# Attention and an MLP in one instruction stream: S2 and S1 score pairs placed one by one between pieces of MLP

## The chip, the cores and the metric

The kernel runs on one core of a Trainium2 chip. The metric is the device time of one execution in microseconds (us). A second time stands beside it: the span, from the first to the last instruction that the hardware profiler recorded in one profiled execution.

The engines are called as in the profile: PE is TensorE (PEld its weight loads, which overlap its matmuls), DVE is VectorE, ACT is ScalarE, POOL is GpSimd, SP is SyncE, which issues most DMAs. Each engine works through its own instruction stream in order; they wait for one another by semaphores.

## The reference, cut to what matters

```python
x: 1 x 2048 x 576 (float32), H = 32 heads of Dh = 18, F = 4608
g = sigmoid((x * gate_w).sum(-1, keepdims=True))

qkv = x @ wqkv                       # 576 -> 3 * 576
scores = q @ k.T * Dh ** -0.5        # per head 2048 x 2048
p = softmax(scores)
a = (p @ v) merged over heads @ wo   # 576 -> 576

y = layernorm(x)
h = gelu(y @ w1 + b1)                # 576 -> 4608, tanh form of gelu
b = h @ w2 + b2                      # 4608 -> 576

out = g * a + (1 - g) * b
```

All matrices are float32. The kernel keeps precision by splitting values into a high part (type fp32r) and the rest; a product is then three matmuls, high by high, high by low and low by high, added up in one PSUM bank.

## The kernel before, in words

There are three stages. First, x is transposed and normalised, and q, k, v are computed and written to DRAM scratch with their high and low parts (up to about 250 us). Second, one long loop does all of attention and, in its gaps, all of the MLP. Third, the output projection with `wo` runs in the gaps of the loop's last steps and after it (from about 2230 us).

**Attention in the loop.** A unit is one pair of heads and one half of the 2048 queries: 32 units. A step is one unit and one block of 128 keys: 16 steps a unit, 512 steps. The loop at line 1113 runs over units and steps. Each step does, twice, for the two blocks of 512 queries:

- S2 (`s2`, matmul at line 250): the scores of 128 keys by 512 queries for both heads, two matmuls on the two halves of PE's rows at once, a *pair*. ACT takes the exponential of each (line 253) into one of three tiles of p (`RING`).
- S1 (`next_round`, `s1_round`, matmul at line 210): a pair of score blocks with queries in the rows, for the *next* unit, of which DVE takes the row maximum (line 212). The maxima enter the next unit's S2 as extra rows of q. S1 runs one unit and 8 rounds ahead, so the last unit has none.

After every second step `pv` (line 268) multiplies the p of two steps by v: 16 matmuls that use PE as four column groups. So two steps, a *double step*, hold four S2 pairs, four S1 pairs and one PV, and there are 256 double steps.

S2 and S1 take their PSUM banks from one round of five (`score_bank`, line 106). Every pair takes two. Numbered in the order of issue, a pair's first bank was the second bank of the pair three before it, and its second bank the first bank of the pair two before it. S2 and S1 alternate, so an S1 waits on its first bank for the exponentials of the S2 three pairs back, and an S2 on its first bank for the reduces of the S1 three pairs back.

**The MLP in the gaps.** The MLP is a Python generator (`mlp`, line 321). It works through 36 groups: 4 blocks of 512 tokens by 9 groups of 512 hidden columns. A group is two `h_pair`s and four `out_pair`s.

- `h_pair` (line 436) computes 2 x 128 hidden columns for 512 tokens: 27 pairs of matmuls (line 460), one on each row half. Then ACT and POOL do the GELU by steps that `defer` and `queue_end` put off (lines 480 to 514).
- `out_pair` (line 518) adds a group's part of the output for 128 tokens: 24 pairs of matmuls (line 538) into two banks of 288 columns. In the first 12 pairs (turn 0) row half 0 writes bank 0 and half 1 writes bank 1; in the last 12 (turn 1) they change banks. Between the turns, the first matmul of turn 1 must not start before the last two of turn 0 have ended. This is done by the `token`: a tiny activation on ACT (line 547) that waits for those two, and for which the first matmul of turn 1 waits. DVE then adds the banks to the accumulator (line 556).

Both generators yield after every matmul pair and set `cut` where a piece ends. `atom` (line 636) takes one piece. `fill` (line 1096) is called three times a double step, with a share of 0, 1 or 2, and takes one piece each time; `piece[0]` tells the generator in which of the three gaps it stands, and the set `ends` holds the pair counts at which it cuts. In `h_pair`, `last` marks the one before a group's outputs; it is stretched over two double steps. `behind` compares the MLP work done (`spent`) with what should be done by this step (`TOTAL`, `FIN`), so that the MLP ends near step 500.

**The order of everything else.** `run_due` (line 143) advances a model clock (`now`) and a call counter (`slot`) and issues what is due: deferred activations, POOL work, DMA issues. It is called eight times in a double step. Nothing is reordered afterwards: the order in which Python emits the instructions is the order on each engine.

In a double step PE gets: S2 S1 PV, S2 S1, gap 0, S2 S1, gap 1, S2 S1, gap 2. `GAP` (1130 ns) is the least time by which the model clock advances in a gap. After the MLP, `fill` calls `filler` with `FILL` (1100 ns) of the projection's matmuls in each gap. `out_proj` issues its preparations at the steps in `PSTEP`, among them `normed` (line 989), DVE and ACT work on the first block of attention outputs, one stage a `run_due` call.

Of the kernel before, what the change touches and what calls it, by code (L numbers as in the profile page):

```python
# [8 lines left out]
F32 = mybir.dt.float32  # L9
# [18 lines left out]
G = 4  # L28
# [12 lines left out]
LAND = 8  # L41
GAP = 1130.0
BUSY = 20
# [17 lines left out]
def gated_mix_kernel(ctx: ExitStack, tc: tile.TileContext, x, wqkv, wo, w1, b1, w2, b2, gate_w, out):  # L61
    nc = tc.nc
# [68 lines left out]
    def defer(n, fn):  # L131
        later.append((slot[0] + n, fn))
# [188 lines left out]
    def mlp():  # L321
# [102 lines left out]
        open_pairs = [0]  # L424
        token = const.tile([1, 1], F32, name="token")

# [9 lines left out]
        def h_pair(q, last, inner=False):  # L436
# [14 lines left out]
            loaded = 0  # L451
            late = spent[0] < behind[0]
            ends = cuts(27, (5, 5, 4)[piece[0]] if last else (3, 5, 4)[piece[0]])
            if last and piece[0] == 0 and not late:

                ends = {4, 9, 14, 18, 23}
            for k, (w_, s_, c) in enumerate(slots):
# [60 lines left out]
        def out_pair(i, t, acc):  # L518
# [4 lines left out]
            ps = [psum(ps_w) for _ in range(2)]  # L523
            ends = {6, 12} if piece[0] == 0 else {12}
            k = 0
            ends_at, seen = [], []
            for turn in range(2):
                for j in ORDER:
                    while (i, j) not in HT:
                        cut[0] = 3  # L530
                        yield 0
                    hh, hl = HT[i, j]
                    w_ = ready(W2, (i * (G // 2) + j // 2, j % 2))
                    for h_, p_ in ((hh, 0), (hh, 1), (hl, 0)):
                        for h in (0, 1) if turn == 0 else (1, 0):
                            r = slice(64 * h, 64 * h + 64)
                            nn = h ^ turn
                            mm = nc.tensor.matmul(ps[nn][:, :ND], h_[r, tok], w_[p_][r, cs[nn]],  # L538
                                                  start=(k == 0), stop=(k == 6 * G - 1))
                            if k == 3 * G - 1:  # L540
                                ends_at.append(mm)
                            elif k == 3 * G:
                                behind_of(mm, seen[0])
                        k += 1
                        if k == 3 * G:

                            seen.append(nc.scalar.activation(token, ident[:1, :1], AF.Copy))  # L547
                            for mm in ends_at:
                                behind_of(seen[0], mm)
                        if k < 6 * G:  # L550
                            if k in ends:
                                cut[0] = 1
                            yield 131
# [76 lines left out]
    cut = [0]  # L630
    piece = [0]
    behind = [0.0]
    hidden = [-1]
# [271 lines left out]
    def out_proj():  # L905
# [134 lines left out]
        for c in range(7):  # L1040
            defer(c, lambda c=c: normed(0, c))
        yield 0
# [52 lines left out]

    def fill(step, share):

        if over[0] is None and not stream and kept[0] == NT and step > PSTEP[-1] + 1:
            stream.append(proj)
            over[0] = step  # L1100
            spent[0] = 0.0
        if over[0] is None:
            piece[0] = share
            behind[0] = base + (TOTAL - base) * step / FIN
            t = spent[0]
            atom()
            run_due(max(spent[0] - t, GAP))
        else:
            filler(spent[0] + FILL)
            run_due()  # L1110

    looped[0] = True
    for u in range(NU):
        for kc in range(NT):
# [17 lines left out]
            s2(u, kc, 0)  # L1132
            next_round()
            run_due(462.0)
            if kc % 2:
                fill(step, 1)
            elif step > 0:
# [4 lines left out]
            s2(u, kc, 1)  # L1142
            next_round()
            run_due(462.0)
            fill(step, 2 if kc % 2 else 0)
    pv(NSTEP - 2)
# [28 lines left out]
```

## Time and profile before

| | |
|---|---|
| time of three runs, us | 2324.1, 2324.93, 2325.55; median 2324.93 |
| profiled execution | 2325.55 us; span 2323.8 us; mean granted clock of PE 0.996 |
| busy time: PE, PEld | 2292.7 us (99%), 1544.4 us (66%) |
| DVE, ACT, POOL | 1664.8 us (72%), 1441.9 us (62%), 967.7 us (42%) |
| S2 matmuls (line 250) | 2048, 454.7 us busy |
| S1 matmuls (line 210) | 2048, 457.9 us busy |
| PV matmuls (line 268) | 2736 and 1360, 345.0 and 179.1 us busy |
| MLP matmuls (lines 460 and 538) | 3888 and 4352 + 2176 (+ 384), 510.4 and 466.3 + 333.8 us busy |
| row maxima on DVE (line 212) | 2048, 1314.8 us, 685 ns each |
| exponentials on ACT (line 253) | 2048, 740.6 + 368.2 us, 594 ns each |
| token on ACT (line 547) | 144, median 202 ns |

How to read it: busy time is the time in which at least one instruction of the group was in its engine. On PE a matmul counts from its start to a modelled end, also while it waits for its weights, so 99% does not say that PE was at its peak; the distances between the starts of matmuls do. A pair of matmuls on the two row halves shows as x2 in a list by time. "idle before" is the time the engine stood before an instruction, with what ended it. The granted clock is the share of full speed at which the throttle let PE run.

### The profile page before, as it was taken

How to read it: one execution, taken by the hardware profiler on the slowest of the kernel's cores; microseconds unless marked ns; L12 is line 12 of the kernel's file. 1: busy time of each engine (PE TensorE's matmuls, PEld its weight loads, DVE VectorE, ACT ScalarE, POOL GpSimd, SP SyncE). 2: the span in 40 equal slices, each digit the busy share in tenths (PEclk: the TensorE clock that was granted, in tenths of full speed). 3: DMA queues.
4: the chain of work that ended last, by engine and by line, in shares of the span. 5: the costliest groups of instructions: out<-in, count | busy, mean ns of one | idle time of the engine just before them, and what ended most of it. 6: DMA issues, size and time to landing. Idle time of an engine off the chain costs nothing.

```text
span 2323.8 us, 51438 instructions
## 1 busy us (share of the span) xinstructions
PE 2292.7 (99%) x20585; PEld 1544.4 (66%) x20585; DVE 1664.8 (72%) x2890; ACT 1441.9 (62%) x2773; POOL 967.7 (42%) x965
## 2 busy tenths in 40 slices
PE   8998999999999999999999999999999999999999
PEld 7876666666666666666666666666666666666658
DVE  5665677777777777777777777777777777777734
ACT  4222577777776666666676666666666666666662
POOL 4001466666564433333353444444434333333700
PEclk9999899999999999999999999999999999999999
DMA  7747855444456524243263424242364233242264
GB/s 245 244 149 232 232 171 147 149 140 146 137 190 167 159 96 118 99 138 111 77 172 136 157 96 130 88 136 96 118 162 152 96 111 107 97 146 96 77 210 161
DMA packets 165022, 330.31 MB, mean 142 GB/s; under 512 B 57190, under 2 KB 84490, under 8 KB 154054
## 3 DMA queue, kind: packets, MB, share of 16 engines
q1 hardware_dynamic: 163162, 323.76, 44.3%
q8 instruction: 162, 2.65, 0.5%
q10 hardware_dynamic: 1620, 3.26, 0.4%
q14 instruction: 78, 0.64, 0.1%
HBM read 234.16 MB, written 96.58 MB: 142 GB/s over the span
## 4 chain that ended last, share of the span: by engine, by line
PE 92%; DVE 3%; DMA 2%; ACT 1%; issue 1%; SPq 1%; POOL 0%; ACTq 0%; DVEq 0%; POOLq 0%
PE ps L268 20%; PE ps L538 20%; PE ps L460 20%; PE ps L250 13%; PE ps L210 12%; PE ps L1071 3%; PE ps L784 3%; PE ps L805 2%; DVE m L212 1%; DMA qk_scr<-hh 1%; DMA p<-in_A_wqkv_dram 0%; PE ps L711 0%; ACT p L253 0%; DMA x<-in_B_w_dram 0%; DVE x L773 0%
## 5 line engine op out<-in xcount | busy, mean ns | idle before, releaser
L212 DVE TENSOR_REDUCE m<-ps 128x1 f32<-128x512 f32 x2048 | 1314.8, 685 | 393.7 <-PE ps L210 372.2
L253 ACT ACTIVATE p<-ps 128x512 f32<-128x512 f32 x1368 | 740.6, 594 | 372.2 <-PE ps L250 361.9
L166 POOL TENSOR_SCALAR zz<-zz 128x512 f32<-128x512 f32 x288 | 178.6, 620 | 819.1 <-ACT zz L513 802.9
L460 PE MATMUL ps<-big,w 64*128 64x512 f32 x3888 | 510.4, 393 | 0.1
L253 ACT ACTIVATE ring<-ps 128x512 f32<-128x512 f32 x680 | 368.2, 594 | 187.6 <-PE ps L250 182.9
L538 PE MATMUL ps<-w,hh 64*128 64x288 f32 x4352 | 466.3, 299 | 4.0 <-ACT token L547 3.5
L210 PE MATMUL ps<-ka,qa 54*128 54x512 f32 x2048 | 457.9, 422 | 11.0 <-DVE hl L736 6.5
L250 PE MATMUL ps<-qa,ka 56*128 56x512 f32 x2048 | 454.7, 423 | 0.7 <-DVE m L212 0.4
L460 PEld LDWEIGHTS ps<-big,w 64*128 64x128 f32 x3888 | 371.4, 185 | 82.3 <-ACT z L481 0.4
L538 PEld LDWEIGHTS ps<-w,hh 64*128 64x128 f32 x4352 | 370.7, 186 | 45.5 <-ACT token L547 17.3
L166 POOL TENSOR_TENSOR zz<-zz,z 128x512 f32<-128x512 f32 x288 | 371.7, 1291 | 24.0
L250 PEld LDWEIGHTS ps<-qa,ka 56*128 56x128 f32 x2048 | 204.3, 184 | 216.6 <-DVE m L212 180.8
L268 PE MATMUL ps<-p,vt 128*32 128x512 f32 x2736 | 345.0, 599 | 0.0
L538 PE MATMUL ps<-w,hl 64*128 64x288 f32 x2176 | 333.8, 293 | 0.0
L210 PEld LDWEIGHTS ps<-ka,qa 54*128 54x128 f32 x2048 | 206.6, 186 | 110.6 <-ACT p L253 42.4
L166 POOL TENSOR_TENSOR w<-x,w 128x576 fp32r<-128x576 f32 (+1 forms) x54 | 98.3, 1836 | 307.2 <-DMA qk_scr<-hh 172.2
L538 PEld LDWEIGHTS ps<-w,hl 64*128 64x128 f32 x2176 | 215.5, 185 | 0.3 <-POOL hl L166 0.3
L166 POOL TENSOR_TENSOR hl<-zz,hh 128x512 fp32r<-128x512 f32 x136 | 176.6, 1299 | 11.3
L268 PE MATMUL ps<-ring,vt 128*32 128x512 f32 x1360 | 179.1, 598 | 0.0
L268 PEld LDWEIGHTS ps<-p,vt 128*32 128x32 f32 x2736 | 71.5, 109 | 161.2 <-issue 153.9
L556 DVE SCALAR_TENSOR_TENSOR x<-ps,x 128x288 f32<-128x288 f32 x256 | 105.1, 452 | 57.3 <-PE ps L538 57.3
L784 PE MATMUL ps<-big,wqk 128*128 128x512 f32 x432 | 109.7, 402 | 1.5 <-POOL wqk L706 1.4
(101 smaller groups left out, 1394.0 us busy)
## 6 DMA issues: line engine op xcount, KB each, us to landing
w<-w_scr SPq DMA_DIRECT2D x54, 1152.0 KB
w<-w_scr SPq DMA_DIRECT2D x108, 576.0 KB
x<-in_B_w_dram SPq DMA_DIRECT2D x72, 288.0 KB
w_scr<-w SPq DMA_DIRECT2D x18, 1152.0 KB
w_scr<-w SPq DMA_DIRECT2D x36, 576.0 KB
big<-y_scr SPq DMA_DIRECT2D x42, 384.0 KB
qa<-qk_scr SPq DMA_DIRECT2D x192, 72.0 KB
ka<-qk_scr SPq DMA_DIRECT2D x84, 144.0 KB
```

The lines of the kernel that those rows point to most:

```text
L166: fn(*args, **kw)
L210: nc.tensor.matmul(ps, qa[r0:r0 + 54, t * P:(t + 1) * P], ka[r0:r0 + 54, kb * TB:(kb + 1) * TB], start=True, stop=True)
L212: nc.vector.tensor_reduce(M4[u][:, h, t, kb:kb + 1], ps, axis=AX.X, op=ALU.max)
L250: nc.tensor.matmul(ps[h], ka[r0:r0 + 56, kc * P:(kc + 1) * P], qa[r0:r0 + 56, qb * TB:(qb + 1) * TB], start=True, stop=True)
L253: nc.scalar.activation(RING[n % 3][:, qb, h], ps[h], AF.Exp, scale=SCALE)
L268: nc.tensor.matmul(OB[u][r:r + 32, :], v[:, k, 19 * h:19 * h + 32], RING[c % 3][:, qb, h, :], start=(k == 0), stop=(k == NT - 1))
L460: nc.tensor.matmul(ps[h], wt[w_][r, c, :], Y[s_][r, c, :], start=(k == 0), stop=(k == 26))
L538: mm = nc.tensor.matmul(ps[nn][:, :ND], h_[r, tok], w_[p_][r, cs[nn]], start=(k == 0), stop=(k == 6 * G - 1))
L556: nc.vector.scalar_tensor_tensor(dst, ps[nn][:, :ND], 0.5, b2b[:, cs[nn]] if g == 0 else dst, op0=ALU.mult, op1=ALU.add)
L784: nc.tensor.matmul(ps, w_[:, c, ms], big[:, s_, :], start=(k == 0), stop=False)
L805: nc.tensor.matmul(ps[:, :ND], big[:, s_, tok], w_[:, c, cs], start=(k == 0), stop=False)
L1071: nc.tensor.matmul(ps[:, :ND], OT[b][2][:, s_, tok], w_part(w_, c)[:, cs], start=(k == 0), stop=(k == 13))
```

## The change

A gap now lies behind every S2 and every S1 pair except the S1 before PV and the S2 and S1 at the turn, so S2 and S1 no longer follow each other directly. A double step has seven gaps, 0 to 6. PE gets: S2, gap 6, S1, PV, S2, gap 0, S1, gap 1, S2, gap 2, S1, gap 3, S2, gap 4, S1, gap 5, and S2, gap 6 again. A new `half_round` does a gap, an S1 round and `run_due`; it stands where `next_round` and `run_due` stood.

An output pair is cut after 3, 6, 12, 18 and 21 of its 24 matmul pairs and skips gap 3 (`skip`), so that the gaps from 0 on hold 3, 3, 6, 0, 6, 3, 3 pairs. The turn lies where gap 3 is empty: an S1 and an S2 pair stand between the turns. Without S1 rounds (the last unit) the cuts are 6, 12, 16, 20 and gaps 2 and 3 are skipped. An output pair that begins in a later gap is cut evenly. An h_pair takes the gaps that are left in its double step, and seven more where it is `last` and the MLP isn't late, or where it doesn't begin in gap 0.

The token is replaced by a semaphore of its own, `swap`: ACT increments it with an instruction that computes nothing and that waits for the last two matmuls of turn 0; PE waits for its value before turn 1 with an instruction of its own.

`run_due` is still called eight times in a double step: in each of the four `half_round`s, after PV, and after gaps 1, 3 and 5. `since` holds the MLP work done up to the last odd gap, by which the model clock is advanced; `GAP` becomes 1000. In `out_proj`, each stage of the first block's `normed` comes three calls later.

```diff
-GAP = 1130.0
+GAP = 1000.0
+GAPS = 7
+TURNS = (3, 6, 12, 18, 21)
+TAIL = (6, 12, 16, 20)
...
-        token = const.tile([1, 1], F32, name="token")
+        swap = tc.alloc_semaphore("swap")
+        swaps = [0]
...
-            late = spent[0] < behind[0]
-            ends = cuts(27, (5, 5, 4)[piece[0]] if last else (3, 5, 4)[piece[0]])
-            if last and piece[0] == 0 and not late:
-
-                ends = {4, 9, 14, 18, 23}
+            left = GAPS - piece[0]
+            skip.clear()
+            if (last and spent[0] >= behind[0]) or left < GAPS:
+                left += GAPS
+            ends = cuts(27, left)
...
-            ends = {6, 12} if piece[0] == 0 else {12}
+            skip.clear()
+            if piece[0]:
+                ends = cuts(24, GAPS - piece[0]) | {12}
+            elif rounds:
+                ends = set(TURNS)
+                skip.add(3)
+            else:
+                ends = set(TAIL)
+                skip.update((2, 3))
             k = 0
-            ends_at, seen = [], []
+            ends_at = []
             for turn in range(2):
+                if turn == 1:
+                    nc.tensor.wait_ge(swap, swaps[0])
...
                             if k == 3 * G - 1:
                                 ends_at.append(mm)
-                            elif k == 3 * G:
-                                behind_of(mm, seen[0])
                         k += 1
                         if k == 3 * G:
 
-                            seen.append(nc.scalar.activation(token, ident[:1, :1], AF.Copy))
+                            seen = nc.scalar.sem_inc(swap, 1)
+                            swaps[0] += 1
                             for mm in ends_at:
-                                behind_of(seen[0], mm)
+                                behind_of(seen, mm)
...
-            defer(c, lambda c=c: normed(0, c))
+            defer(c + 3, lambda c=c: normed(0, c))
...
-    def fill(step, share):
+    def fill(step, gap):
...
-            piece[0] = share
+            piece[0] = gap
             behind[0] = base + (TOTAL - base) * step / FIN
-            t = spent[0]
-            atom()
-            run_due(max(spent[0] - t, GAP))
-        else:
+            if gap not in skip:
+                atom()
+        elif gap % 2:
             filler(spent[0] + FILL)
-            run_due()
+            since[0] = spent[0]
+        if gap % 2:
+            run_due(max(spent[0] - since[0], GAP))
+            since[0] = spent[0]
+
+    def half_round(step, gap):
+
+        fill(step, gap)
+        next_round()
+        run_due(462.0 + spent[0] - since[0] if gap == GAPS - 1 else 462.0)
+        if gap == GAPS - 1:
+            since[0] = spent[0]
...
             s2(u, kc, 0)
-            next_round()
-            run_due(462.0)
+            half_round(step, 2 if kc % 2 else GAPS - 1)
             if kc % 2:
-                fill(step, 1)
+                fill(step, 3)
             elif step > 0:
                 pv(step - 2)
                 while ROWS:
                     ROWS.pop(0)()
                 run_due(2080.0)
             s2(u, kc, 1)
-            next_round()
-            run_due(462.0)
-            fill(step, 2 if kc % 2 else 0)
+            half_round(step, 4 if kc % 2 else 0)
+            fill(step, 5 if kc % 2 else 1)
```

More of the change, by code (lines that the diff above doesn't have):

```diff
@@ L631, in gated_mix_kernel @@
     piece = [0]
+    skip = set()
+    since = [0.0]
     behind = [0.0]
@@ L1100, in fill @@
             over[0] = step
-            spent[0] = 0.0
+            spent[0] = since[0] = 0.0
         if over[0] is None:
-            piece[0] = share
+            piece[0] = gap
             behind[0] = base + (TOTAL - base) * step / FIN
-            t = spent[0]
-            atom()
-            run_due(max(spent[0] - t, GAP))
-        else:
+            if gap not in skip:
+                atom()
+        elif gap % 2:
             filler(spent[0] + FILL)
-            run_due()
+            since[0] = spent[0]
[8 more added lines that the diff above has]
+            since[0] = spent[0]
     looped[0] = True
```

## The prediction

> **What bounds the kernel now.** I read the page first, then TensorE's weight loads and what they waited for, then seven double steps in a row by window, then one double step instruction by instruction. "PEld" is a weight load, "idle before" the time its unit stood.
>
> ```profile
> span 2323.8 us, 51438 instructions
> PE 2292.7 (99%) x20585; PEld 1544.4 (66%) x20585; DVE 1664.8 (72%) x2890; ACT 1441.9 (62%) x2773; POOL 967.7 (42%) x965
> ```
>
> TensorE bounds the span, but its 99% counts a matmul that stands in the pipe behind a late weight load. Losses must be read from the distances between starts. These are the waits of weight loads from 300 to 2200 us:
>
> ```profile
> PEld ps L210 <- ACT p L253: 41.5, 159, 1.4
> PEld ps L210 <- ACT ring L253: 18.7, 73, 0.3
> ...
> PEld ps L538 <- ACT token L547: 12.5, 64, 0.3
> ...
> PEld ps L210 <- DVE m L212: 5.1, 14, 0.4
> ```
>
> S1 (L210) waits for the exponentials of the S2 pair before it (L253): five score banks go round, S2 and S1 take two each, so S1's first bank is the second bank of the S2 three pairs earlier. The exchange token (L547) is next. VectorE hardly holds TensorE. Seven consecutive double steps (a whole group of MLP: h_pair in one step, h_pair in two, four output steps):
>
> ```profile
> 2082.30:2092.51 10.21, 10.21 (x88) 6.91 (x87) 5.72 (x11) 4.51 (x9) 0.00 (x0) 1.00 0.56 221
> 2092.51:2099.74 7.23, 7.23 (x63) 4.41 (x61) 6.23 (x10) 6.81 (x14) 4.92 (x6) 1.00 0.25 67
> 2099.74:2106.83 7.09, 7.09 (x60) 4.22 (x58) 5.27 (x9) 4.64 (x9) 6.48 (x7) 1.00 0.49 186
> 2106.83:2114.21 7.38, 7.38 (x82) 5.00 (x81) 5.99 (x12) 6.78 (x15) 5.20 (x6) 1.00 0.45 161
> 2114.21:2121.66 7.45, 7.45 (x82) 5.00 (x80) 5.90 (x12) 4.50 (x10) 6.18 (x7) 1.00 0.06 22
> 2121.66:2129.18 7.52, 7.52 (x83) 5.01 (x81) 5.87 (x12) 4.51 (x10) 0.00 (x0) 1.00 0.01 2
> 2129.18:2136.69 7.51, 7.51 (x82) 5.01 (x81) 6.21 (x15) 4.49 (x10) 0.00 (x0) 1.00 0.00 0
> ```
>
> Columns: length, then busy us of PE, PEld, DVE, ACT, POOL, then granted clock (1.00), DMA share, GB/s. An output step takes 7.38 to 7.52 us, mean 7.465, whatever POOL and DMA do; DVE is busy 5.9 to 6.2 us of it, ACT 4.5 to 6.8. Inside the step from 2121.66, TensorE's starts:
>
> ```profile
> 2121.31 0.43 PE L210 MATMUL ps<-ka,qa 54*128 54x512 f32 x2
> 2121.66 1.06 PE L268 MATMUL ps<-ring,vt 128*32 128x512 f32 x8
> ...
> 2123.52 0.50 PE L250 MATMUL ps<-qa,ka 56*128 56x512 f32 x2
> 2123.86 0.40 PE L210 MATMUL ps<-ka,qa 54*128 54x512 f32 x2
> 2124.09 0.43 PE L538 MATMUL ps<-w,hh 64*128 64x288 f32 x4
> ...
> 2124.89 0.40 PE L250 MATMUL ps<-qa,ka 56*128 56x512 f32 x2
> 2125.25 0.50 PE L210 MATMUL ps<-ka,qa 54*128 54x512 f32 x2
> 2125.59 0.43 PE L538 MATMUL ps<-w,hh 64*128 64x288 f32 x4
> ...
> 2126.25 0.30 PE L538 MATMUL ps<-w,hl 64*128 64x288 f32 x2
> 2126.38 0.40 PE L250 MATMUL ps<-qa,ka 56*128 56x512 f32 x2
> 2126.61 0.41 PE L210 MATMUL ps<-ka,qa 54*128 54x512 f32 x2
> 2126.90 0.54 PE L538 MATMUL ps<-w,hh 64*128 64x288 f32 x4
> ...
> 2128.59 0.42 PE L250 MATMUL ps<-qa,ka 56*128 56x512 f32 x2
> ...
> ```
>
> A free S2 or S1 pair takes 0.23 us to the next start (2126.38 to 2126.61), six output pairs 0.79 (2125.59 to 2126.38), so 0.132 each. Four distances are longer than that: S2 to S1 0.36 at 2124.89 (0.13 lost), S1 to output 0.34 at 2125.25 (0.11 lost, because the load after a late load comes late too), S1 to output 0.29 at 2126.61 (0.06, the token), twelve pairs in 1.69 for 1.59 (0.10, again the pair after a late load). Sum 0.40. Without them the step is 7.52 - 0.40 = 7.12. The entry into PV (0.35) and the way out of it (0.34) are in the 7.12 and stay, since PV still has S1 ahead and S2 behind it.
>
> **The change, part by part.** *Same work.* No matmul, exponential or reduce is added or removed. Output pieces go from 6, 6, 12 to 3, 3, 6, 0, 6, 3, 3; h pieces from 9, 9, 9 to seven of 3 or 4, and to fourteen of about 2 where an h_pair gets two double steps. An MLP pair costs the same 0.13 or 0.23 beside S2 and S1 as beside itself, so more borders cost 0; a border at which each side paid 0.01 would cost 8 x 0.01 x 256 = 20 us, and the h steps, at most 0.07 over their pairs in two of three, bound it well under that.
>
> *S1's wait for the exponentials.* The rows:
>
> ```profile
> 2124.29 1.29 DVE L212 TENSOR_REDUCE m<-ps 128x1 f32<-128x512 f32 x2 [1.00 <-PE ps L210]
> ...
> 2125.25 0.19 PEld L210 LDWEIGHTS ps<-ka,qa 54*128 54x128 f32 x2 [0.30 <-ACT p L253]
> ...
> 2125.39 1.08 ACT L253 ACTIVATE ring<-ps 128x512 f32<-128x512 f32 x2 [0.18 <-PE ps L250]
> ...
> 2126.65 0.20 ACT L547 ACTIVATE token<-ident 1x1 f32<-1x1 f32 x1 [0.18 <-PE ps L538]
> ...
> 2126.90 0.30 PEld L538 LDWEIGHTS ps<-w,hh 64*128 64x128 f32 x4 [0.18 <-ACT token L547]
> ```
>
> An S2 is used up 0.50 + 1.08 = 1.58 us after its start (2124.89, 2125.39), and S1 sees it 0.05 later: 1.63, or some 0.1 more behind PV. Now S1 is due 0.34 + 0.23 + 0.80 + 0.23 = 1.60 after that S2, its load 0.13 earlier, so it is late. With lone pairs the distance is four pairs and twelve output pairs less one pair: 3 x 0.23 + 12 x 0.132 = 2.27, load due at 2.14. That leaves about 0.4 to 0.5 us, enough for nothing to wait, and nearly enough for one GELU activation between (mean 0.64, L513 in the fence on the exchange). These 0.24 us go.
>
> *What is late next: S2 behind the reduces.* S2's first bank is the second of the S1 three pairs back. A reduce pair starts 0.43 after S1 (2123.86, 2124.29) and takes 1.29, seen 0.05 later: 1.77. In the new order two S2 of a double step (the one at the turn and the one after the last gap) follow that S1 by 2 x 0.23 + 0.40 + 0.79 + 0.23 = 1.88, load due at 1.75. So both are level with VectorE, within 0.02. A late load costs 0.1 by the row at 2125.59. Bounds: 0 (level means in time) and 0.3 (both, and S1 after the output's accumulation). I take 0.13: more often in time than not, with one late load a step.
>
> *Exchange.* 144 token activations leave ACT (36 groups x 4 output pairs, x144 below) and an increment and a TensorE wait take their place; neither is in the trace.
>
> ```profile
> L547 ACT ACTIVATE token<-ident x144: 185/202/204, 294.3 to 2228.4; 1x1 f32<-1x1 f32 x144
> L547 ACTq EVENT_SEMAPHORE  x105: 17/17/17, 301.7 to 2227.8; - x105
> ...
> L538 PEldq EVENT_SEMAPHORE  x81: 51/51/356, 794.6 to 2203.5; - x81
> ...
> L513 ACT ACTIVATE zz<-z 128x512 f32<-128x512 f32 x138 | 80.0, 640 | 1.5 <-DVE z L480 1.3
> ```
>
> The increment costs 0.017 (nearest kind) to 0.20 (the token). The twelfth pair started at 2126.25 and the token 0.40 later; by the 0.017 row an answer is back about 0.40 + 0.02 + 0.05 = 0.47 after that start. The next output pair is due 0.13 + 0.23 + 0.23 = 0.59 after it, its load at 0.46: level. TensorE's own wait is 0.051, hidden while S1 and S2 stream; exposed it costs 144 x 0.051 = 7 us. What stands behind the wait is all of TensorE: six pairs, S1d, the next S2 and PV. Behind the increment on ACT stand the next S2's exponentials, which are due 0.5 us later anyway. But ahead of it now stand the exponentials of the S2 that opens the 6-pair gap: they end 1.58 after that S2, while the twelfth pair starts at 0.23 + 5 x 0.132 = 0.89. If the increment waits for their end, it goes at 0.69 and is back at 0.76 after the twelfth pair, 0.30 late. Ends: 0 and 0.30; I take 0.02, by the 17 ns row, which is a sequencer's entry beside the activations and not among them. The Trainium skill, "Perfetto Trace Analysis", per-engine timelines, gives a sequencer-only instruction no place in the engine's FIFO, so the increment need not outlast an exponential; by that the sum stays. The Trainium skill, "TensorE: Matmul & The Clock Gate", on engine queue depths, calls ACT's queue a strict FIFO; if that holds the increment back, rival 1 follows. No row of this profile decides between them.
>
> *Sum of output steps.* (7.465 - 7.12 - 0.15) x 144 = 0.195 x 144 = 28 us.
>
> *h steps.* By the same distances an h step is 0.35 + 1.86 + 0.34 + 6 x 0.23 = 3.93 and 0.231 a pair: 10.17, 7.16, 6.93 for 27, 14, 13 pairs; the windows show 10.21, 7.23, 7.09, so 0.27 a group, x 36 = 10. I take half: 5.
>
> *First MLP pass and end.*
>
> ```profile
> 442.19:450.20 8.01, 7.98 (x62) 4.59 (x61) 5.60 (x9) 7.69 (x16) 5.79 (x6) 1.00 0.27 110
> 479.64:487.75 8.11, 8.09 (x83) 5.18 (x81) 5.89 (x12) 5.21 (x11) 2.65 (x1) 1.00 0.31 127
> 2208.03:2214.75 6.72, 6.45 (x74) 4.32 (x72) 0.82 (x3) 4.24 (x9) 0.75 (x1) 1.00 0.55 185
> 2221.47:2231.65 10.18, 7.46 (x75) 5.13 (x73) 4.72 (x9) 6.45 (x13) 0.74 (x1) 0.89 0.67 218
> ```
>
> While ACT still splits weights, two steps of a group take 0.78 and 0.60 more than later ones (8.01 for 7.23, 8.11 for 7.51); some 8 groups, 11 us. The wider distance hides about half: 5. In the last unit S1 is gone: four pairs and 24 output pairs ask 6.16 (7.12 less four S1 of 0.24), three steps take some 0.56 more and one 4.0 more, in which the token stands behind late activations of the projection. Halving the first and moving the projection's normalisation three calls later save 4 of these 5.7.
>
> The DMA issues and POOL calls come from run_due, called eight times a double step before and after, so SP's and POOL's order stays; POOL is idle in two of the seven windows, which covers shifts of a microsecond. If that cover went, an output pair would wait for its GELU and lose its place in the gaps.
>
> Sum: 28 + 5 + 5 + 4 = 42. The profiled execution took 2325.55 us (span 2323.8), 0.6 above the median 2324.93. 2325.55 - 42 = 2283.5; I say 2283.
>
> **The rivals.**
> 1. *The answer is held by the exponentials*: 0.30 at each turn. That stall also gives VectorE time, so the S2 waits shrink to 0.05: (0.345 - 0.35) x 144 = 0, and 14 remain from the other terms: 2311. For it: token and exponentials share ACT today. Against: the 17 ns row.
> 2. *Slower: S2 waits for VectorE.* Place: the two S2 1.88 behind their S1, and the S1 behind the accumulation (L556). It decides from a loss of 0.345 + 14/144 = 0.44 a step, that is three late loads with VectorE only 0.05 behind each time. At 0.1 behind, 3 x 0.2 = 0.6 a step: 2325.5 + (0.6 - 0.345) x 144 - 14 = 2348. For it: VectorE has 6.2 us of work in 7.12. Against: the 1.86 us of PV let it catch up once a step.
> 3. *Everything goes*: residue 0, h 10, pass 11, end 6: 2325.5 - 50 - 27 = 2249.
> 4. *It does not do what it says*: gains are given back elsewhere, 2320 to 2330.
>
> **How the numbers follow.** Forecast (2268 to 2297) 0.50, since its two unknowns are both level; rival 3 (below 2268) 0.12; rival 1 (2297 to 2320) 0.18; rival 4, within 0.2% (4.6 us, about what a measurement can tell from nothing), 0.06; rival 2 0.14. Faster 0.50 + 0.12 + 0.18 = 0.80, same 0.06, slower 0.14. The range 2256 to 2328 leaves out rival 2 and the better half of rival 3, 0.20.
>
> **What would show it.** Right: S1's weight loads wait under 10 us for ACT, output steps of 7.2 to 7.35, S2's loads waiting for VectorE in place of it. The turn: an output load right at S2's start plus 0.1. Wrong: output loads waiting 0.3 behind an exponential (rival 1), S2 waits of 0.2 or more on L212 in every step (rival 2), output pairs that start in a gap other than the first, or a new wait for GELU.

## The result and the profile after

The changed kernel takes 2288.47 us (median of five runs, 2287.58 to 2289.88); the kernel before took 2325.55 us beside it (2324.1 to 2326.21). The ratio is 0.9842, with a 95% interval of 0.9828 to 0.9855: 37 us are gone, where 42 were forecast. Where one execution of a kernel stands far above its others at a lower granted clock (2440.14 us at 0.849 in e10, 2365.27 at 0.924 in the kernel before), the times below leave it out. The profiled execution has a span of 2286.4 us. Its totals, by engine:

```profile
span 2286.4 us, 51621 instructions
...
PE 2248.4 (98%) x20585; PEld 1592.3 (70%) x20585; DVE 1649.0 (72%) x2890; ACT 1416.4 (62%) x2629; POOL 967.4 (42%) x965
```

TensorE has the same 20585 matmuls, and ACT has 144 instructions less (2773 to 2629), the tokens. As before, the totals do not say where the time went. A group of MLP near the end does: the same seven double steps as in the prediction, in windows cut at the starts of PV (length; PE, PEld, DVE, ACT, POOL busy; granted clock, DMA share, GB/s).

```profile
2048.00:2058.21 10.21, 10.21 (x91) 6.92 (x90) 5.90 (x12) 4.57 (x10) 0.00 (x0) 1.00 0.53 213
2058.21:2065.41 7.20, 7.20 (x65) 4.72 (x63) 6.49 (x10) 6.21 (x13) 5.38 (x6) 1.00 0.24 60
2065.41:2072.48 7.07, 7.07 (x63) 4.56 (x61) 5.05 (x8) 4.67 (x9) 6.03 (x7) 1.00 0.51 193
2072.48:2079.63 7.15, 7.15 (x83) 5.21 (x82) 5.72 (x11) 6.50 (x14) 4.98 (x6) 1.00 0.48 166
2079.63:2086.77 7.14, 7.14 (x84) 5.18 (x83) 5.78 (x11) 4.84 (x11) 6.45 (x7) 1.00 0.06 23
2086.77:2093.90 7.13, 7.13 (x85) 5.16 (x83) 5.77 (x11) 4.28 (x9) 0.00 (x0) 1.00 0.01 2
2093.90:2101.04 7.14, 7.14 (x85) 5.22 (x83) 5.77 (x11) 4.41 (x10) 0.00 (x0) 1.00 0.00 0
```

The four output steps (the last four rows) take 7.13 to 7.15 us where they took 7.38 to 7.52. The three h steps have hardly moved (10.21, 7.20, 7.07 for 10.21, 7.23, 7.09). The waits of weight loads from 300 to 2160 us (total, number, longest) say what is left:

```profile
PEld ps L253 <- DVE m L215: 178.0, 212, 1.5
...
PEld ps L213 <- ACT p L256: 2.4, 3, 1.1
...
PEld ps L552 <- ACTq L559: 1.4, 4, 0.8
```

S1's wait for exponentials (L213, L256) fell from 60 us to 2.4, and loads wait for the exchange (L559) four times in this window. The 178.0 us of the first row are, but for two loads, the load that follows PV; the kernel before has 175.9 in the same row, which the prediction's list leaves out, and the semaphore kernel in the old order, below, has 176.0. The row names VectorE, but the time belongs to PV: in the last unit, where no reduce is left, the start behind that S2 is just as late (0.34, from 2178.93 to 2179.27).

At a turn, TensorE's starts are now these:

```profile
2089.98 0.39 PE L253 MATMUL ps<-qa,ka 56*128 56x512 f32 x2
2090.21 0.42 PE L552 MATMUL ps<-w,hh 64*128 64x288 f32 x4
...
2090.88 0.30 PE L552 MATMUL ps<-w,hl 64*128 64x288 f32 x2
2091.01 0.40 PE L213 MATMUL ps<-ka,qa 54*128 54x512 f32 x2
2091.25 0.39 PE L253 MATMUL ps<-qa,ka 56*128 56x512 f32 x2
2091.48 0.43 PE L552 MATMUL ps<-w,hh 64*128 64x288 f32 x4
```

Every distance is the free one: 0.23 or 0.24 behind S2 and S1, 0.13 a pair. The same turn on the weight loads and on ACT:

```profile
2091.28 0.40 PEld L552 LDWEIGHTS ps<-w,hh 64*128 64x128 f32 x4
```

```profile
2090.47 1.09 ACT L256 ACTIVATE ring<-ps 128x512 f32<-128x512 f32 x2 [0.18 <-PE ps L253]
```

The load that waits for the increment starts at 2091.28, while the exponentials of the S2 that opened the gap run until 2091.56. So the increment did not stand behind them.

Summed over the whole trace (distances between starts of PV; a "regular" output step holds one whole output pair and no transposition and is shorter than 7.7 us):

| steps | before | after |
|---|---|---|
| regular output steps | 113, mean 7.456 | 113, mean 7.137 |
| output steps with a transposition | 17, mean 8.145 | 17, mean 8.022 |
| h steps, all | 105, 875.2 us | 105, 874.0 us |
| from the last S1 step to the end | 129.9 us | 129.1 us |

The first row alone is 0.319 x 113 = 36 us.

### The profile page after: what moved, and what is told of

It reads as the page before. It is cut to its first block, busy times and chain, and to the rows that moved or that the text cites. A ratio compares the mean times of both kernels' runs of the same rounds, so it can differ in the third digit from the quotient of the medians.

```text
span 2286.4 us, 51621 instructions
## 1 busy us (share of the span) xinstructions
PE 2248.4 (98%) x20585; PEld 1592.3 (70%) x20585; DVE 1649.0 (72%) x2890; ACT 1416.4 (62%) x2629; POOL 967.4 (42%) x965
## 4 chain that ended last, share of the span: by engine, by line
PE 89%; DVE 4%; DMA 3%; ACT 2%; issue 1%; SPq 1%; POOL 0%; ACTq 0%; DVEq 0%; POOLq 0%
PE ps L271 20%; PE ps L552 19%; PE ps L464 19%; PE ps L253 12%; PE ps L213 11%; PE ps L799 3%; PE ps L1086 2%; PE ps L820 2%; DVE m L215 2%; ACT p L256 1%; DMA qk_scr<-hl 1%; DMA p<-in_A_wqkv_dram 1%; DMA den<-ot_scr 0%; PE ps L726 0%; DMA x<-in_B_w_dram 0%
## 5 line engine op out<-in xcount | busy, mean ns | idle before, releaser
L256 ACT ACTIVATE p<-ps 128x512 f32<-128x512 f32 x1368 | 741.1, 596 | 399.9 <-PE ps L253 394.7
L464 PE MATMUL ps<-big,w 64*128 64x512 f32 x3888 | 584.9, 393 | 0.8 <-DVE z L484 0.6
L256 ACT ACTIVATE ring<-ps 128x512 f32<-128x512 f32 x680 | 368.9, 597 | 198.5 <-PE ps L253 196.0
L552 PE MATMUL ps<-w,hh 64*128 64x288 f32 x4352 | 486.2, 294 | 3.9 <-DVE x L569 1.3
L253 PE MATMUL ps<-qa,ka 56*128 56x512 f32 x2048 | 464.3, 423 | 6.3 <-ACT p L256 3.3
L213 PE MATMUL ps<-ka,qa 54*128 54x512 f32 x2048 | 448.7, 402 | 10.1 <-DVE hl L751 5.5
L552 PEld LDWEIGHTS ps<-w,hh 64*128 64x128 f32 x4352 | 424.7, 186 | 32.2 <-DVE x L569 3.3
L464 PEld LDWEIGHTS ps<-big,w 64*128 64x128 f32 x3888 | 381.2, 187 | 75.8 <-DVE z L484 1.1
L253 PEld LDWEIGHTS ps<-qa,ka 56*128 56x128 f32 x2048 | 210.4, 184 | 229.5 <-DVE m L215 183.0
L552 PE MATMUL ps<-w,hl 64*128 64x288 f32 x2176 | 349.6, 292 | 0.0
L213 PEld LDWEIGHTS ps<-ka,qa 54*128 54x128 f32 x2048 | 227.0, 185 | 44.5 <-DVE m L215 11.0
L552 PEld LDWEIGHTS ps<-w,hl 64*128 64x128 f32 x2176 | 232.3, 185 | 0.2
```

The source lines that it names most:

```text
L213: nc.tensor.matmul(ps, qa[r0:r0 + 54, t * P:(t + 1) * P], ka[r0:r0 + 54, kb * TB:(kb + 1) * TB], start=True, stop=True)
L253: nc.tensor.matmul(ps[h], ka[r0:r0 + 56, kc * P:(kc + 1) * P], qa[r0:r0 + 56, qb * TB:(qb + 1) * TB], start=True, stop=True)
L256: nc.scalar.activation(RING[n % 3][:, qb, h], ps[h], AF.Exp, scale=SCALE)
L464: nc.tensor.matmul(ps[h], wt[w_][r, c, :], Y[s_][r, c, :], start=(k == 0), stop=(k == 26))
```

## The experiments

Each kernel is the changed one with one edit, save e2, which is the kernel before with one, and e9, e11 and e12, which have more. Ratios are to the kernel before, run beside it on the same chip.

**The order alone, and the exchange alone.** The first keeps the token in the new order, the second puts the semaphore into the old one.

```diff
 # e1: the new order with the token
-                if turn == 1:
-                    nc.tensor.wait_ge(swap, swaps[0])
+                            elif k == 3 * G:
+                                behind_of(mm, seen)
...
-                            seen = nc.scalar.sem_inc(swap, 1)
-                            swaps[0] += 1
+                            seen = nc.scalar.activation(token, ident[:1, :1], AF.Copy)
```

> The changed kernel with the seven gaps, but the token activation on ACT in place of the semaphore (TensorE's first matmul of turn 1 waits for the token, as before). Theory (the gain has two parts, and the semaphore is the one that lets the turn go without a wait): the token lies behind the exponentials of the S2 that opens the 6-pair gap; they end 1.58 us after that S2, the token 0.2 later, and the load of turn 1 is due at 1.35, so each of 144 turns loses 0.2 to 0.4 us: 2317 to 2346 us, and output steps of 7.35 to 7.55 us. Rival (the lone pairs alone make the gain; the S1 and S2 pair between the turns hide either exchange): 2285 to 2292 us, output steps still 7.13.

> The kernel before with its three gaps, but the exchange by semaphore. Theory (two parts): the loss at the turn, 0.06 + 0.10 us in each of 144 output pairs, goes, S1's wait of 0.24 stays: 23 us less at most, 2302 to 2310 us, output steps 7.3. Rival (only the order matters): 2322 to 2328 us. Together with the run before this makes a table of order by exchange; if the two parts simply add up, the four times fit to within 5 us.

e1 took 2327.15 us, ratio 1.0009 (1.0 to 1.0019), as its theory says. e2 took 2310.51, ratio 0.9933 (0.9918 to 0.9948), half a microsecond above its theory's range. Two steps of e1 by window, then the rows of its loads' waits that answer to the exchange:

```profile
2109.47:2116.84 7.37, 7.37 (x82) 5.12 (x81) 5.88 (x11) 6.54 (x15) 5.18 (x6) 1.00 0.45 161
2116.84:2124.22 7.38, 7.38 (x83) 5.11 (x81) 5.81 (x11) 4.96 (x12) 6.22 (x7) 1.00 0.06 22
```

```profile
PEld ps L549 <- ACT token L558: 48.9, 135, 2.8
```

And e2's rows for S1:

```profile
PEld ps L210 <- ACT p L253: 43.1, 163, 1.4
PEld ps L210 <- ACT ring L253: 19.2, 74, 0.3
```

| | token | semaphore |
|---|---|---|
| old order | 2325.9 | 2310.5 |
| new order | 2327.2 | 2288.5 |

The order alone gives nothing, the semaphore alone 15 us, both together 37: the parts do not add. The distances inside a regular output step say why (mean ns over the free distance, which is 231 behind an S2 or S1 and 131 behind an output pair):

| | before | e1 | e2 | after |
|---|---|---|---|---|
| at the turn: to the first output pair, and the pair after it | 50 + 97 | 168 + 107 | 33 + 4 | 2 + 4 |
| S1's wait for exponentials, and the pair after it | 95 + 105 | 1 + 3 | 97 + 106 | 1 + 5 |

In the new order the token stands behind the exponentials of the S2 that opens the 6-pair gap, so e1 pays at the turn (275 ns for 147) most of what it saves at S1 (4 for 200). Its regular step is 7.394, 0.06 shorter than before, which makes some 7 us. It loses them again in single steps: 3.5 us up to 320 us, and 5 in one step of 12.93 (8.12 before), where the token stands behind a weight split that waits 3.20 us for its load. The changed kernel meets that wait too, below. e2 saves at the turn and leaves S1's wait as it was. Of the changed kernel's 37 us, 15 come with the exchange alone, and the other 22 with the new order, on the condition that no activation on ACT answers the exchange. `GAP`, which the change also lowers, was not tried alone; in the regular steps nothing is left for it to explain.

**The increment behind the exponentials (rival 1 by force).**

```diff
+            last_exp[0] = nc.scalar.activation(RING[n % 3][:, qb, h], ps[h], AF.Exp, scale=SCALE)
...
                                 behind_of(seen, mm)
+                            behind_of(seen, last_exp[0])
```

> The changed kernel in which the increment on ACT also waits, by ACT's own semaphore, for the end of the last exponential issued before it. Theory (the increment passes exponentials that still run): the answer comes 0.30 us late at each turn, 0.25 to 0.45 with the pair behind it: 144 x that, 2324 to 2353 us. Rival (ACT holds the increment back already, in order): no change, 2285 to 2292 us.

2322.03 us, ratio 0.9986 (0.9976 to 0.9995): 33.5 us slower than the changed kernel, 2 us under the theory's range and far from the rival's. Its row in the waits of loads:

```profile
PEld ps L553 <- ACTq L560: 49.6, 135, 5.6
```

This is e1's row again (48.9 us, 135 times), and the turn of a regular step loses 166 + 107 ns. So in the changed kernel the increment passes running exponentials, 0.23 us a turn (33.5 / 144). By the Trainium skill, "Perfetto Trace Analysis", per-engine timelines, a sequencer-only instruction has no place in the engine's FIFO; this run agrees. The strict FIFO of the Trainium skill, "TensorE: Matmul & The Clock Gate", engine queue depths, did not hold the increment back.

**How much room VectorE leaves S2, and ACT the exchange.** e4 brings the turn's S2 one output pair nearer to the S1 whose reduces free its bank; e5 spaces the pairs evenly; e8 puts three output pairs into the empty gap (3, 3, 6, 3, 3, 3, 3), so that a single S1 covers the exchange.

```diff
 # e4
-TURNS = (3, 6, 12, 18, 21)
+TURNS = (4, 7, 12, 18, 21)
 # e5
+TURNS = (4, 8, 12, 16, 20)
 # e8
+TURNS = (3, 6, 12, 15, 18, 21)
-                skip.add(3)
```

> The changed kernel with output pairs cut at 4, 7, 12, 18, 21 in place of 3, 6, 12, 18, 21: gaps of 4, 3, 5, 0, 6, 3, 3. The S2 at the turn follows the S1 whose bank it takes by 0.13 us less. If the prediction's sum is right that this S2 is level with VectorE's reduces (load due 1.75, bank free 1.77), its load is now 0.13 to 0.15 late and the next one too: 0.15 to 0.25 us a step, 2308 to 2325 us, with a wait of S2's loads for L215. Rival (VectorE has room there): 2285 to 2293 us.

> The changed kernel with output pairs cut at 4, 8, 12, 16, 20: gaps of 4, 4, 4, 0, 4, 4, 4. Theory (each pair needs its distance): the S2 at the turn and the S2 after the last gap follow the S1 whose bank they take by 0.13 us less than in the changed kernel, and the S1 after gap 4 follows its S2 by 0.53 less, 1.75 us, its load due at 1.62 against a bank free at 1.63. Two or three late loads of 0.11 in each of 144 steps: 32 to 48 us over the changed kernel, less what one stall saves the next: 2305 to 2335 us. Rival (lone pairs are enough, whatever the sizes): 2286 to 2294 us.

> The changed kernel with output pairs cut at 3, 6, 12, 15, 18, 21 and no gap skipped: gaps of 3, 3, 6, 3, 3, 3, 3, so that one S1 pair alone stands at the turn. Theory: the answer is back 0.47 after the twelfth pair started, the load of turn 1 is now due at 0.23: 0.24 late and 0.11 for the pair behind, 0.35 x 144 = 50 us: 2325 to 2345 us, with output steps of 7.45 to 7.5. Rival (the answer comes earlier than that sum says): under 2310 us.

e4 took 2299.46 us, ratio 0.988 (0.9864 to 0.9897), 11 more than the changed kernel and between the two expectations. Its regular output step is 7.237; the turn's S2 starts 15 ns late, and the output pair behind it 105 ns late. The wait row:

```profile
PEld ps L253 <- DVE m L215: 196.7, 332, 1.4
```

That is 120 more loads that wait (332 for 212). The turn's S2 load and the reduces in this kernel, on the weight loads and on VectorE:

```profile
2098.55 0.19 PEld L253 LDWEIGHTS ps<-qa,ka 56*128 56x128 f32 x2 [0.17 <-DVE m L215]
```

```profile
2097.21 1.29 DVE L215 TENSOR_REDUCE m<-ps 128x1 f32<-128x512 f32 x2 [1.11 <-PE ps L213]
```

The reduces end at 2098.50 and the load starts 0.05 later. In the changed kernel the same pair of rows reads

```profile
2091.12 0.19 PEld L253 LDWEIGHTS ps<-qa,ka 56*128 56x128 f32 x2
```

```profile
2089.78 1.29 DVE L215 TENSOR_REDUCE m<-ps 128x1 f32<-128x512 f32 x2 [0.99 <-PE ps L213]
```

There too the load starts 0.05 after the reduces' end, with no idle time shown. Over the 111 regular steps of the changed kernel it starts 0.053 after that end (10 to 90%: 0.052 to 0.053) and 1.776 after S1 (2089.35 to 2091.12 here): VectorE releases the turn's S2 in every step, and this load still leads its matmul by 0.12. In e4 the lead is 0.002. So there was no room at all: a load that is just level costs nothing, and one that is late by one output pair (0.13) costs 0.015 at its own matmul and 0.105 at the next.

e5 took 2316.73 us, ratio 0.9961 (0.9947 to 0.9974), and its regular output steps average 7.383, as its theory says; its row of S2 loads that wait for VectorE has 329 where the changed kernel's has 212. Lone pairs in even gaps are not enough; what counts is the distance of each S2 and S1 from the pair whose bank it takes.

e8 took 2305.75 us, ratio 0.9914 (0.99 to 0.9927): it loses 17 us, less than the theory asked and inside the rival's range. Its turn:

```profile
2101.43 0.31 PE L551 MATMUL ps<-w,hl 64*128 64x288 f32 x2
2101.56 0.41 PE L213 MATMUL ps<-ka,qa 54*128 54x512 f32 x2
2101.84 0.53 PE L551 MATMUL ps<-w,hh 64*128 64x288 f32 x4
2102.21 0.29 PE L551 MATMUL ps<-w,hl 64*128 64x288 f32 x2
```

Its load, from the weight loads:

```profile
2101.84 0.30 PEld L551 LDWEIGHTS ps<-w,hh 64*128 64x128 f32 x4 [0.20 <-ACTq L558]
```

The twelfth pair starts at 2101.43 and the answered load 0.41 later, at the same time as its matmul. With S1 at 2101.56 the load was due at 2101.56 + 0.24 - 0.13 = 2101.67: it is 0.17 late. S1 to output is 0.28 for 0.24, so only 0.04 of that is paid at once, and 0.11 at the pair behind (0.37 for 0.26). The load's lead of 0.13 takes the rest. So the time is that of an answer that comes early, and it does come early by 0.06 (0.41 for 0.47), but the greater part is the lead. In the changed kernel the answered load starts 0.40 after the twelfth pair too (2090.88 to 2091.28; median over the regular steps 0.394, of which the increment's start is at 0.329), where it was due at 0.47 by its matmul. So the answer leaves 0.07.

**The end and the first pass.** e7 moves the projection's normalisation back to where it was; e6 issues ACT's split of a weight two calls later after the weight's load.

```diff
 # e7
-            defer(c + 3, lambda c=c: normed(0, c))
+            defer(c, lambda c=c: normed(0, c))
 # e6
-LAND = 8
+LAND = 10
```

> The changed kernel with the projection's first normalisation at its old calls (not three later). The prediction gave the three calls about 2.5 us by keeping the exchange from standing behind late activations. By that: 2290 to 2293 us, with a turn near the end that waits 2 to 3 us. Rival (the wait for the same loads only moves): 2287 to 2290 us.

> The changed kernel with LAND 10 for 8: while the MLP's weights are split, ACT's split is issued two calls later after its load. The changed kernel's ACT waited once 3.3 us for such a load (at 527 us) with TensorE behind it, and the clock fell for 3.4 us. Theory (shorter steps make the loads late): that stall of about 4 us goes: 2282 to 2287 us. Rival (weights come too late for h_pair instead, or the loss sits elsewhere): 2288 to 2296 us.

e7 took 2287.56 us, ratio 0.9835 (0.9821 to 0.9848): the three calls are worth nothing that can be measured. What holds the end of the changed kernel shows on VectorE, ACT and TensorE:

```profile
2208.92 0.69 DVE L1012 TENSOR_TENSOR x<-x,den 128x512 f32<-128x512 f32 x1 [6.52 <-DMA den<-ot_scr]
```

```profile
2209.70 0.63 ACT L1015 ACTIVATE big<-x 128x512 fp32r<-128x512 f32 x1 [5.25 <-DVE x L1012]
2210.23 3.02 ACT L256 ACTIVATE p<-ps 128x512 f32<-128x512 f32 x6
```

```profile
2210.86 0.50 PE L253 MATMUL ps<-qa,ka 56*128 56x512 f32 x1 [1.60 <-ACT p L256]
```

The normalisation of a later block waits 6.5 us for its load; ACT's share of it waits 5.25 us for VectorE; six exponentials queue behind that, and S2 waits for them. The step takes 11.33 us (8.72 in e7, where the same load is waited for). In the last unit no turn waits in either kernel: the output steps there take 6.19 us at most, but for the one with a transposition.

e6 took 2290.23 us (2287.14 to 2293.83), ratio 0.9843 (0.983 to 0.9857), inside the rival's range. It was aimed at the costliest step of the changed kernel's first pass, 11.83 us from 523.9, here by window (three pieces), on TensorE, and on ACT:

```profile
523.90:530.10 6.20, 5.06 (x52) 2.95 (x49) 4.83 (x10) 1.86 (x4) 5.14 (x6) 1.00 1.06 181
530.10:533.40 3.30, 2.08 (x17) 1.44 (x19) 0.81 (x2) 2.48 (x4) 1.23 (x1) 1.00 0.79 313
533.40:536.80 3.40, 3.40 (x25) 2.28 (x27) 1.90 (x4) 1.72 (x4) 1.42 (x1) 0.50 0.13 30
```

```profile
530.11 0.49 PE L253 MATMUL ps<-qa,ka 56*128 56x512 f32 x1 [1.15 <-DVE m L215]
531.13 0.53 PE L552 MATMUL ps<-w,hh 64*128 64x288 f32 x4 [0.53 <-ACTq L559]
```

```profile
530.92 1.17 ACT L373 ACTIVATE w<-x 128x1152 fp32r<-128x1152 f32 x1 [3.30 <-DMA x<-in_B_w_dram]
531.99 2.04 ACT L256 ACTIVATE p<-ps 128x512 f32<-128x512 f32 x4
```

ACT's split of a weight waits 3.30 us for the weight to land; exponentials queue behind it, and so does the increment: the row of 531.13 waits for it. An increment passes an activation that runs, but not the wait of one that stands ahead of it: that wait is a row of ACT's sequencer (L373, at 530.84), and the increment follows it (531.06). With the split two calls later the 3.3 us wait and a step of 11.68 are there just the same. The trace shows the delay before the landing: SP needs 4.38 us (from 521.32) to issue the first of the weight's two loads, where most of these loads take 0.6 to 0.7, so the second goes out only at 525.75; in e6 it is 5.32 us. What holds SP there is not shown, and this place remains open.

**Steps with a transposition.** The 17 output steps with a transposition (L230) gained 0.12 us, where the others gained 0.32. Two kinds lose. In the first, ACT's copy of the transposed maxima (L232) waits for TensorE while a square and four exponentials queue behind it:

```profile
1057.03 0.27 ACT L232 ACTIVATE mr<-ps 32x128 fp32r<-32x128 f32 x1 [0.69 <-PE ps L230]
1057.20 1.14 ACT L517 ACTIVATE zz<-z 128x512 f32<-128x512 f32 x2
1058.25 2.00 ACT L256 ACTIVATE p<-ps 128x512 f32<-128x512 f32 x4
```

In the second, three small operations of `s1_finish` (L224 to L226) and the end of an output delay VectorE's reduces (those of the S1 at 1115.53 start only at 1118.00), and one S1 of a pair comes late, here on VectorE and then on TensorE:

```profile
1116.76 0.59 DVE L226 TENSOR_TENSOR nm<-nm,nmh 128x16 f32<-128x16 f32 x1
...
1118.00 2.56 DVE L215 TENSOR_REDUCE m<-ps 128x1 f32<-128x512 f32 x4
```

```profile
1117.72 0.28 PE L230 MATMUL ps<-ident,nm 128*32 128x128 f32 x1
...
1118.73 1.10 PE L213 MATMUL ps<-ka,qa 54*128 54x512 f32 x2
...
1119.84 0.39 PE L253 MATMUL ps<-qa,ka 56*128 56x512 f32 x1
...
1120.07 0.39 PE L253 MATMUL ps<-qa,ka 56*128 56x512 f32 x1
```

From there the two row halves of the array run out of step (pairs show as x1 and x1). Four more kernels went after these steps: e9 gives the three small operations to POOL, with the transposition one double step later; e10 gives the copy L232 to VectorE; e11 does both; e12 is e11 with the transfers of the maxima into q on SP's queue alone.

```diff
 # e9 (in the loop; the rest as before)
-        nc.vector.tensor_copy(nmh, nm)
-        nc.vector.tensor_copy(nm2[:, :, 0, :], nmh.bitcast(F32))
-        nc.vector.tensor_tensor(nm2[:, :, 1, :], nm, nmh.bitcast(F32), op=ALU.subtract)
+            nc.gpsimd.tensor_scalar(nmh, nm, 1.0, 1.0, op0=ALU.mult, op1=ALU.mult)
+            nc.gpsimd.tensor_scalar(nm2[:, :, 0, :], nmh.bitcast(F32), 1.0, 1.0, op0=ALU.mult, op1=ALU.mult)
+            nc.gpsimd.tensor_tensor(nm2[:, :, 1, :], nm, nmh.bitcast(F32), op=ALU.subtract)
...
-            ROWS.append(rows)
+            NEXT.append(rows)
 # e10 (in the loop)
-            nc.scalar.activation(mr, ps[:32, :P], AF.Copy)
+            nc.vector.tensor_copy(mr, ps[:32, :P])
 # e12, over e9 and e10
-            queue = nc.scalar if looped[0] and slot[0] - inflow[0] < BUSY else nc.sync
+            queue = nc.sync
```

> The changed kernel, in which the end of a unit's row maxima (three small operations after the maximum, some 1.1 us of VectorE) runs on POOL and the transposition of the maxima comes one double step later. Theory (the steps with a transposition lose 0.7 us more than their own 0.21 because VectorE's reduces come late there, S1's second matmul at 1118.7 us waits for them): the second output steps of this kind fall from 8.10 to about 7.45 us, the first ones stay at 8.00, their loss being ACT's: 2 to 4 us in all, 2284 to 2287 us. Rival (the loss is the transposition itself, or ACT's copy of it): 2287 to 2291 us.

> The changed kernel with the copy of the transposed maxima (0.27 us) on VectorE in place of ACT. Theory (in the first output step of a group ACT's squares wait behind this copy, which waits for TensorE, and the next S2's exponentials start 0.74 us late): steps of that kind fall from 8.00 to about 7.4 us, six of them, 3 to 5 us: 2283 to 2286 us. Rival (VectorE has no room for it and its own reduces come late): 2288 to 2293 us.

> Both edits together. Theory (two separate causes): the gains add, 2280 to 2285 us, and every step with a transposition takes 7.35 to 7.5 us. Rival: no better than the better of the two alone.

> The kernel with both edits, in which the two DMAs that store the maxima into q always go out on SyncE's queue (in the others they go out on ACT's while the next block's inputs load, hold ACT's queue 2.08 us, and TensorE then waits 2.5 us for exponentials at 1189 us, in a step of 11.82). Theory (that step's loss is the DMA issue on ACT): it falls to about 7.4 us, 2277 to 2281 us. Rival (on SyncE's queue they stand behind the loads and land late, and the next unit's S2 waits): 2284 to 2300 us, with a wait of S2 for a DMA.

| | time | ratio | output steps with a transposition, sum of 17 |
|---|---|---|---|
| changed kernel | 2288.47 | 0.9842 (0.9828 to 0.9855) | 136.4 |
| e9 | 2285.81 | 0.9838 (0.9825 to 0.9852) | 133.3 |
| e10 | 2284.25 | 0.9826 (0.9813 to 0.984) | 134.8 |
| e11 | 2283.35 | 0.9823 (0.981 to 0.9837) | 130.6 |
| e12 | 2289.45 | 0.9849 (0.9833 to 0.9866) | 138.3 |

In e9, e11 and e12 the transposition falls into other double steps, so their 17 are compared by kind: the first is the first output step of a group, the second its second one. e9 takes the second kind from 8.10 to between 7.33 and 7.39 us (in the second output step and in the third, to which these transpositions move) and leaves the first at 8.00; e10 takes the first to between 7.35 and 7.42 and leaves the second at about 8.1. So the first kind has the cause named. For the second, e9 excludes the transposition itself, but it makes two edits, and which of them helps is not told apart. By their times none of the three is clear of the changed kernel: e11 is the fastest of this study by its median, some 5 us below it, and the intervals overlap. In e11 all these steps take 7.33 to 7.37 us but two, of 8.55 (from 1675.7) and of 11.82, the latter on ACT and TensorE:

```profile
1187.74 2.08 ACTq L127 DMA_DIRECT2D qa<-mr  x2
```

```profile
1191.55 0.49 PE L258 MATMUL ps<-qa,ka 56*128 56x512 f32 x1 [2.47 <-ACT p L261]
```

Two DMA issues hold ACT for 2.08 us, and TensorE stands 2.47 for exponentials. e12 was to save that. It moved the wait to the transfer instead, as its rival says: TensorE's waits from 260 to 2150 us, and the stretch from 1191.4:

```profile
PE ps L258 <- DMA qa<-mr: 11.4, 2, 9.1
```

```profile
1191.40:1200.90 9.50, 2.26 (x10) 1.69 (x10) 0.29 (x1) 1.47 (x3) 1.14 (x1) 0.50 0.68 157
```

S2 waits 9.1 us for the maxima, one step takes 17.98, and the granted clock is down to 0.5. ACT's queue was the cheaper one here.

## Why the prediction was right

2283 was forecast and 2288.47 measured, within the forecast's own 2268 to 2297. The sign, the place and the mechanism held; the terms came out as follows.

- **Output steps, 28 us: measured about 36 in the regular ones and 2 in those with a transposition.** The distance argument held almost exactly: without late loads the step was to be 7.12, and is 7.137. What failed is the residue of 0.15 (0.13 for S2 behind the reduces, 0.02 for the exchange); measured it is 0.02. The time in it was right to a hundredth: the reduces are seen 1.77 after S1 by the prediction, 1.776 by the trace. The choice between the ends 0 and 0.3 was not: "level" was priced as one late load a step, and a level load costs 0. The steps with a transposition were not treated apart in the prediction, and gained 0.12 each.
- **Exchange, back at 0.47 with the load due at 0.46: measured 0.39.** The increment goes 0.33 after the twelfth pair's start, not 0.42; the token's 0.40 in the trace of before was taken for the matmul's share, and the trace now shows 0.33.
- **Rival 1, the answer held by exponentials: excluded** by the load at 2091.28 and by e3, which costs what the rival described. The place was right too: 0.69 and 0.76 after the twelfth pair were forecast for a held increment and the load behind it, 0.645 and 0.733 are e3's medians. The price of 2311 was too low, because a few turns lose over 0.54 at their first pair (the longest wait is 5.6 us) and the other 14 us were not there: e3 ends at 2322.
- **Rival 2, S2 waiting for VectorE: did not come, but there is no room before it.** VectorE releases the turn's S2 in every regular step; one output pair nearer costs 11 us (e4).
- **Rivals 3 and 4** did not come. Output steps went to the floor as rival 3 says, but its other terms did not.
- **h steps, 5 us: measured about 2** (22 groups behind the first pass: 0.02 and 0.07 us in the steps of 14 and 13 pairs, none in those of 27; 0.09 x 22 = 2). The way from the free distances to 10.17, 7.16 and 6.93 does not fit h pairs; they stay at 10.22, 7.21 and 7.06 with no wait to show for it.
- **First MLP pass, 5 us: less than nothing.** Its h steps of 14 pairs fell from 8.01 to 7.77 (7 x 0.24 = 1.7). Its heavy output steps fell from 8.11 to 7.85, a little less than a regular step does, so the wider distance hid none of ACT's weight splits there. The step at 523.9 lost another 4.0 (11.83 for 7.85).
- **End, 4 us: measured 0.8.** Steps without S1 fell from 6.72 to 6.19 as worked out, and the one of 10.18 fell to 6.19 too. But it does so in e7 as well, so the some 3 us credited to the three later calls were not theirs; and the six projection steps that follow took 49.7 us for 45.0, since ACT waits there behind the load of `den` and holds exponentials in place of the token.

So the total was near in part by luck: one term was 10 us too small (38 for 28) and three were too large by some 13 together (h 3, first pass 7, end 3). Added up, these measured terms make 39 us of the 37.4 by which the span fell; the rest lies in single steps outside them.

## What to carry to other kernels

Read the loss from distances between starts, not from busy time: a late weight load costs what its lead of 0.13 us does not cover, and about 0.11 us again at the load behind it, so that two causes made 0.35 us of a 7.45 us step. Ask of each of two changes made together whether one removes what the other runs into; here the new order was worth nothing with the token and 22 us with the semaphore. An answer to TensorE went faster here by an increment that no activation has to run for, but check what may stand and wait ahead of it.

## What was not expected of the hardware

- ACT's increment passes running activations (e3: +33.5 us without it) but stood behind the wait of an activation for a DMA (TensorE stood 0.53 us at 531.13).
- One late matmul of a row-tiled pair puts the two halves of the array out of step: the second S1 of the pair of 1118.73 starts 0.60 us after the first, and the step is 0.7 to 0.8 longer than its like in e9.
- The price of a late load rises almost at once: 0.01 late (the turn's S2 of the changed kernel) costs 0.006 + 0.002, 0.13 late (e4) 0.015 + 0.105, 0.17 late (e8) 0.044 + 0.106, some 0.27 late (e3) 0.15 + 0.11 in the median, at its own matmul and at the next.
- A stretch in which TensorE was busy for 7.14 of 9.50 us (from 523.9), with no single stand longer than the 1.15 us at 530.11, was followed by 3.4 us at a granted clock of 0.50; in e12 the clock stayed at 0.5 for 13.65 us.
- Two small DMA issues on ACT's queue hold it for 2.08 us (1187.74 in e11).
